# Spectral filter beside a Mish layer: eviction order and PSUM banks of the first layer

## The chip, the core and the metric

The kernel runs on one core of one Trainium2 chip. The metric is the device time of one execution in microseconds. A core has five engines, each with its own instruction queue: PE (TensorE, matmuls; PEld is its loading of weights), DVE (VectorE), ACT (ScalarE), POOL (GpSimd) and SP (SyncE, which here only issues DMAs). Matmul results land in PSUM, 128 partitions of 8 banks of 512 float32 each. ACT and DVE read them from there into SBUF.

## The reference

Two branches work on x (1 x 2048 x 512, bf16) and a gate mixes them.

```python
g = sigmoid((x * gate_w).sum(-1, keepdims=True))
X = rfft2(x.astype(float32), axes=(-2, -1)) * (w_r + 1j * w_i)      # branch A
a = irfft2(X, s=(2048, 512), axes=(-2, -1)).astype(bfloat16)
h = einsum("bsd,df->bsf", x, w1) + b1                               # branch B, F = 1792
act = h * tanh(softplus(h))                                         # mish
b = einsum("bsf,fd->bsd", act, w2)
return g * a + (1 - g) * b
```

## The kernel before

**Branch A** does the two-dimensional Fourier transform as matmuls, 2048 = 64 x 32 along the rows. The steps on PE, in the order of their dependence: transposes of x (`tr`, L507 to L528), a transform along the columns (`a1`, L588 to L591), the first half of the row transform (`s1`, L609, four of them). Its result goes out to a scratch tensor in HBM and comes back in another layout (`r1w`, `r1r`, DMAs on SP). Then four rounds n = 0 to 3 of `s2` (L727, second half of the row transform), a complex product with the filter on DVE (`wm`, L738) and a combination on POOL or DVE (`wz`, L744), and `s2i` (L780, the first half of the inverse transform). A small extra step, `s2x` (L693 to L695), handles one frequency column: DVE copies and adds (`rs`, L700; `x0`), then a row of small POOL operations ends in `z0` and the copies `wc_n` (L770), which each `s2i` needs. The results of `s2i` are evicted (`e4`, helper at L439 on DVE and L440 on ACT) and go through HBM again (`r2w`, 8 DMAs; `r2r`, 8 DMAs). For each of 16 row tiles t, then: `s1i` (L811), an eviction `e5` (L439 or L440, into `misc`), `a1i` (L823), a scaling by the gate on ACT (`geo`, L828) and two sums (`ga`, L831).

**Branch B** is a layer of F = 14 blocks of 128 over four groups c of 512 rows. `layer1(c, ft)` is one unit: four matmuls of 128x512 into one PSUM bank (L565), then a mish with bias on ACT (L575) into `act[:, c % 3, ft, :]`. There are 56 units. The second layer, `mm2` (L879; L862 for the last tile), takes 14 matmuls per row tile, in two halves of seven, into banks 4 and 5 in turn. It is evicted by ACT for the first 12 tiles (L837, with the gate as a per-partition scale), and by DVE for the others (`fin`, L889 and L869).

**PSUM banks.** Branch A uses banks 0 to 3 (and 4 and 5 in `s1`; `rcw`, L658, a small correction to the filter, uses 5). Layer 1 takes banks 6 and 7 in turn; the unit (0, 2) alone takes bank 5. A unit can start when the mish that reads its bank's former contents is done.

**Row order.** x is loaded with row 16p + t on partition p of tile t, and the transposes apply a permutation (`perm`) so that the two halves of 64 columns of a tile hold even and odd partitions. The mish restores the order: it reads the bank in order and writes its output with a step of two elements. `e5` does the same for branch A.

**Order.** No order is written out by hand. Every step is a task with an engine (or a choice of two), a planned duration, what it reads and writes, and a priority. A list scheduler (`_Graph.schedule`) plays them through at build time: of the tasks that could start within 0.1 us of the earliest, it takes the one with the highest priority, then the longest remaining path. The order on each engine's queue comes from that, and so do the waits (semaphores). For a DMA, the planned transfer time is bytes over the argument `bw`; this changes the plan alone, not the transfer. Each engine's queue is then strictly in order on the chip.

Of the kernel before, what the change touches and what calls it, by code (L numbers as in the profile page):

```python
# [14 lines left out]
NFT = 14  # L15
# [288 lines left out]

NBF = 12
NWARM = 40
PR = dict(sp0=95.0, mm1c0=90.0, mm1c=88.0, mish=92.0, mm2=70.0, fin=94.0, gate=60.0, sum=60.0)


def _build(nc, A_x, A_w_r, A_w_i, B_x, B_w1, B_b1, B_w2, gate_w, out):  # L310
# [11 lines left out]
    with es:  # L322
# [7 lines left out]
        act = sb("act", [128, 3, NFT, 512], BF)  # L330
# [221 lines left out]
                tt(f"t2{t}", Tb[:, 1, t0:t0 + 2, :], yy[:, 0], yy[:, 1], ALU.subtract, 256, [("y", yi)], [("T2", t0), ("T2", t)])  # L552


        n_mm1 = [0]

        def layer1(c, ft):
            hb, prio = c % 3, PR['mm1c0'] if c == 0 else PR['mm1c'] - c
            bank = 5 if (c, ft) == (0, 2) else 6 + n_mm1[0] % 2
            n_mm1[0] += bank != 5  # L560

            def f_mm1(e, ds):
                ins = None
                for dt_ in ds:
                    ins = e.matmul(ps[:, bank, :], w1_sb[:, dt_, 128 * ft:128 * (ft + 1)], xT[:, dt_, 4 * c:4 * c + 4, :], start=(dt_ == 0), stop=(dt_ == 3))  # L565
                return ins

            for ds in (((0,), (1,), (2,), (3,)) if (c, ft) in early else ((0, 1, 2, 3),)):
                t_mm1 = pe(f"mm1_{c}_{ft}_{ds[0]}", len(ds) * mm(512), lambda e, ds=ds: f_mm1(e, ds), writes=[("bank", bank)],
                           reads=[("xT", 4 * c + i, dt_) for i in range(4) for dt_ in ds] + [("w1", ft)],  # L570
                           prio=PR['mm1c0'] + 8 - ft if (c, ft) in early else prio)
                if (c, ft, ds[0]) == (0, 0, 0):
                    G.filled = t_mm1
            G.add(f"mish_{c}_{ft}", "act", act_dur(512, True),
                  lambda e: e.activation(act[:, hb, ft, :].rearrange("p (t a b) -> p t b a", t=4, b=2), ps[:, bank, :].rearrange("p (t b a) -> p t b a", t=4, b=2),  # L575
                                         AF.Mish, bias=b1f[:, ft:ft + 1]),
                  reads=[("bank", bank), "b1f"], writes=[("act", hb, ft)], prio=PR['mish'])

# [102 lines left out]
        s2_tasks = []  # L681
# [114 lines left out]
        for tq in range(8):  # L796
            b0 = 4 * tq
            dma(f"r2r{tq}", T2r[:, b0:b0 + 4, :], scr2_r[:, b0:b0 + 4, :],
                reads=[("scr2", n, h) for n in range(4) for h in range(2)], writes=[("T2r", b0 + i) for i in range(4)],
                deps=s2_tasks[-1:], nbytes=128 * 2048)  # L800
        G.cur_prio = SP0 + 2.6
        for t in range(NT):
            bank, ts_, gb = t % 2, t % 4, t % 2

            def f_s1i(e, t=t, bank=bank):
                ptt = ps[:, bank, :].rearrange("p (bx kc n) -> p bx kc n", bx=2, kc=2)
                ins = None
                for bx in range(2):
                    b = 2 * t + bx
                    for kc in range(2):  # L810
                        ins = e.matmul(ptt[:, bx, kc, :], T2r[:, b, 128 * kc:128 * (kc + 1)], G1s[:, b, :], start=True, stop=True)  # L811
                return ins

            pe(f"s1i_{t}", 4 * mm(128), f_s1i, reads=[("T2r", 2 * t), ("T2r", 2 * t + 1), ("m1", 0), ("m1", 1)], writes=[("bank", bank)])
            evict(f"e5_{t}", 512, TT[:, ts_, :, :].rearrange("p j (a b) -> p j b a", b=2),
                  ps[:, bank, :].rearrange("p (b j a) -> p j b a", b=2, j=4), [("bank", bank)], [("TT", ts_)])

            yk = 2 + t % 2

            def f_a1i(e, ts_=ts_, yk=yk):  # L820
                ins = None
                for j in range(4):
                    ins = e.matmul(ps[:, yk, 256 * (j // 2):256 * (j // 2) + 256], TT[:, ts_, j, :], GDs[:, j, :], start=(j % 2 == 0), stop=(j % 2 == 1))  # L823
                return ins

            pe(f"a1i_{t}", 4 * mm(256), f_a1i, reads=[("TT", ts_), "GD"], writes=[("bank", yk)])
            G.add(f"geo_{t}", "act", act_dur(512, True),
                  lambda e, t=t, gb=gb, yk=yk: e.activation(gEO[:, gb, :], ps[:, yk, :], AF.Copy, scale=gcol[:, t:t + 1]),  # L828
                  reads=[("bank", yk), "gcol"], writes=[("gEO", gb)])
            for (i, op) in ((0, ALU.add), (1, ALU.subtract)):  # L830
                fg = (lambda e, i=i, op=op, t=t, gb=gb: e.tensor_tensor(out=ga[:, t, 256 * i:256 * i + 256], in0=gEO[:, gb, 0:256], in1=gEO[:, gb, 256:512], op=op))  # L831
                G.add_multi(f"ga{i}_{t}", [("dve", dve_dur(256), fg), ("pool", pool_dur(256), fg)],
                            reads=[("gEO", gb)], writes=[("ga", t, i)])
# [10 lines left out]

        for c in range(NCH):
            hb = c % 3
            for ft in range(NFT):
                if (c, ft) not in early:
                    layer1(c, ft)
            G.cur_prio = PR['mm2'] - c  # L850
            for tl in range(4):
                t = 4 * c + tl
                bank = 4 + (t % 2)
                if t == NT - 1:
                    G.cur_prio = PR['mm2'] - 10
                    for i, (c0, w_) in enumerate(((0, 384), (384, 128))):
                        cs_, bk = slice(c0, c0 + w_), 1 + i

                        def f_mm2h(e, t=t, tl=tl, bk=bk, hb=hb, cs_=cs_, w_=w_):
                            ins = None  # L860
                            for ft in range(NFT):
                                ins = e.matmul(ps[:, bk, 0:w_], act[:, hb, ft, 128 * tl:128 * (tl + 1)], w2_sb[:, ft, cs_],  # L862
                                               start=(ft == 0), stop=(ft == NFT - 1))
                            return ins

                        pe(f"mm2_{t}_{i}", 14 * mm(w_), f_mm2h, reads=[("act", hb, ft) for ft in range(NFT)] + [("w2", 0), ("w2", 1)],
                           writes=[("bank", bk)])
                        G.add(f"fin_{t}_{i}", "dve", dve_dur(w_, True),
                              lambda e, t=t, bk=bk, cs_=cs_, w_=w_: e.scalar_tensor_tensor(out=xo[:, t, cs_], in0=ps[:, bk, 0:w_], scalar=omg[:, t:t + 1],  # L869
                                                                                    in1=ga[:, t, cs_], op0=ALU.mult, op1=ALU.add),  # L870
                              reads=[("bank", bk), "omg", ("ga", t, 0), ("ga", t, 1), ("x", t)], writes=[("o", t, i)], prio=PR['fin'])
                        dma(f"out{t}_{i}", ov[:, t, cs_], xo[:, t, cs_], reads=[("o", t, i)], nbytes=128 * 2 * w_, is_out=True,
                            queue=("sp", "act")[i], prio=PR['fin'])
                    continue
                for part in range(2):
                    def f_mm2(e, t=t, tl=tl, bank=bank, part=part, hb=hb):
                        ins = None
                        for ft in range(7 * part, 7 * part + 7):
                            ins = e.matmul(ps[:, bank, :], act[:, hb, ft, 128 * tl:128 * (tl + 1)], w2_sb[:, ft, :],  # L879
                                           start=(ft == 0), stop=(ft == NFT - 1))  # L880
                        return ins

                    pe(f"mm2_{t}_{part}", 7 * mm(512), f_mm2,
                       reads=[("act", hb, ft) for ft in range(7 * part, 7 * part + 7)] + [("w2", part)], writes=[("bank", bank)])
                if t < NBF:
                    evict_b(t, bank)
                else:
                    G.add(f"fin_{t}", "dve", dve_dur(512, True),
                          lambda e, t=t, bank=bank: e.scalar_tensor_tensor(out=xo[:, t, :], in0=ps[:, bank, :], scalar=omg[:, t:t + 1],  # L889
                                                                           in1=ga[:, t, :], op0=ALU.mult, op1=ALU.add),  # L890
                          reads=[("bank", bank), "omg", ("ga", t, 0), ("ga", t, 1)], writes=[("x", t), ("o", t)], prio=PR['fin'])
                    if t == NT - 2:
                        store(t, t + 1)
                    elif t % 2 == 1:
                        store(t - 1, t + 1)
# [113 lines left out]
```

## Time and profile before

| | |
|---|---|
| runs, median (lowest to highest) | 141.21 us (140.84 to 141.6, three runs) |
| profiled execution: time | 141.44 us |
| profiled execution: span, first to last instruction | 139.7 us |
| granted TensorE clock, mean | 1.000 |
| PE busy | 132.9 us (95%) |
| PEld busy | 67.3 us (48%) |
| DVE busy | 87.6 us (63%) |
| ACT busy | 88.3 us (63%) |
| POOL busy | 36.7 us (26%) |

The page gives, for one execution, each engine's busy time, and the chain of work that ended last: followed back from the last instruction, at each step to what released it. By engine that chain is PE 78%, ACT 11%, DMA 6%, issue 2%, DVE 1%. "Issue" is time in which an engine waited for nothing that the profile shows. A group of instructions is given as its line, engine, operation, output and input tiles, shapes and count, then after the bar its busy time in us and the mean of one in ns, then the engine's idle time just before them and what ended most of it. A busy PE isn't PE at its best: matmuls are pipelined, so one of 512 columns is shown as 380 ns although they follow one another every 0.216 us.

Busy time by stretch (us from the start of the span; PE, DVE and ACT busy us):

| stretch | what runs | PE | DVE | ACT |
|---|---|---|---|---|
| 8.50 to 38.85 | tr, a1, s1; units 3 to 22 of layer 1 | 29.98 of 30.35 | 22.50 | 28.85 |
| 38.85 to 60.47 | units to 43; s2_0, s2x | 20.69 of 21.62 | 14.46 | 17.48 |
| 60.47 to 75.95 | s2i_0 to s2_2; mm2 of group 0 | 15.16 of 15.48 | 10.03 | 5.54 |
| 75.95 to 88.38 | the last 12 units; s2i_2, s2_3 | 12.13 of 12.43 | 9.62 | 10.45 |
| 93.07 to 103.88 | s2i_3, mm2, the road through HBM | 9.69 of 10.81 | 1.23 | 3.09 |
| 103.88 to 126.75 | s1i, a1i, mm2 | 22.66 of 22.87 | 20.32 | 16.90 |
| 126.75 to 139.70 | the last mm2, fins, stores | 10.56 of 12.95 | 4.60 | 0.82 |

### The profile page before, as it was taken

How to read it: one execution, taken by the hardware profiler on the slowest of the kernel's cores; microseconds unless marked ns; L12 is line 12 of the kernel's file. 1: busy time of each engine (PE TensorE's matmuls, PEld its weight loads, DVE VectorE, ACT ScalarE, POOL GpSimd, SP SyncE). 2: the span in 40 equal slices, each digit the busy share in tenths (PEclk: the TensorE clock that was granted, in tenths of full speed). 3: DMA queues.
4: the chain of work that ended last, by engine and by line, in shares of the span. 5: the costliest groups of instructions: out<-in, count | busy, mean ns of one | idle time of the engine just before them, and what ended most of it. 6: DMA issues, size and time to landing. Idle time of an engine off the chain costs nothing.

```text
span 139.7 us, 2549 instructions
## 1 busy us (share of the span) xinstructions
PE 132.9 (95%) x955; PEld 67.3 (48%) x971; DVE 87.6 (63%) x195; ACT 88.3 (63%) x124; POOL 36.7 (26%) x68
## 2 busy tenths in 40 slices
PE   6999999999999999999999999999969999999993
PEld 4646656655433333433433333434436676665452
DVE  0265777939999259436947947921005999998042
ACT  4289898989989878751066897533137679773000
POOL 2000494030000655234404404400002442673000
DMA  4999999999553956106004106003469321211021
GB/s 97 322 384 382 394 264 283 254 368 338 135 136 113 320 187 225 75 0 155 0 0 115 35 5 152 0 0 83 147 197 292 112 77 75 80 75 75 0 105 47
DMA packets 18920, 21.32 MB, mean 153 GB/s; under 512 B 1180, under 2 KB 16284, under 8 KB 18524
## 3 DMA queue, kind: packets, MB, share of 16 engines
q1 hardware_dynamic: 17872, 17.19, 39.7%
q0 software_dynamic: 864, 3.94, 9.6%
q8 instruction: 7, 0.11, 0.4%
q10 hardware_dynamic: 172, 0.04, 0.1%
q14 instruction: 5, 0.04, 0.1%
HBM read 14.87 MB, written 6.29 MB: 151 GB/s over the span
## 4 chain that ended last, share of the span: by engine, by line
PE 78%; ACT 11%; DMA 6%; issue 2%; DVE 1%; SPq 0%
PE ps L565 27%; PE ps L879 26%; ACT act L575 8%; PE ps L823 5%; DMA Abuf<-scr 3%; PE ps L497 3%; PE ps L609 3%; PE ps L811 3%; DMA scr<-Ybuf 2%; PE ps L862 2%; PE ps L591 2%; PE ps L528 2%; PE ps L727 2%; PE ps L780 1%; ACT Ybuf L440 1%
## 5 line engine op out<-in xcount | busy, mean ns | idle before, releaser
L565 PE MATMUL ps<-xT,w_sb 128*128 128x512 bf16 x215 | 53.2, 380 | 1.5 <-issue 0.3
L575 ACT ACTIVATE act<-ps,b1f 128x512 bf16<-128x512 f32 x56 | 46.3, 837 | 7.0 <-PE ps L565 5.7
L879 PE MATMUL ps<-w_sb,act 128*128 128x512 bf16 x203 | 46.8, 379 | 0.6 <-issue 0.2
L565 PEld LDWEIGHTS ps<-xT,w_sb 128*128 128x128 bf16 x224 | 19.2, 98 | 28.3 <-ACT act L575 10.7
L879 PEld LDWEIGHTS ps<-w_sb,act 128*128 128x128 bf16 x210 | 20.0, 98 | 23.4 <-issue 1.7
L738 DVE TENSOR_TENSOR misc<-ps,WT 128x512 f32<-128x512 f32 x32 | 19.8, 680 | 7.8 <-PE ps L727 7.8
L837 ACT ACTIVATE xo<-ps,omg 128x512 bf16<-128x512 f32 x12 | 8.2, 687 | 18.6 <-PE ps L879 18.6
L831 POOL TENSOR_TENSOR Tg<-misc 128x256 bf16<-128x256 f32 x12 | 10.1, 846 | 26.4 <-ACT misc L828 26.4
L744 POOL TENSOR_TENSOR misc<-misc 128x255 bf16<-128x255 f32 x16 | 11.3, 729 | 19.8 <-DVE misc L738 19.8
L439 DVE CAST Ybuf<-ps 128x512 bf16<-128x512 f32 (+1 forms) x10 | 8.8, 901 | 10.6 <-PE ps L780 9.1
L831 DVE TENSOR_TENSOR Tg<-misc 128x256 bf16<-128x256 f32 x20 | 13.4, 699 | 0.8 <-ACT misc L828 0.8
L439 DVE CAST misc<-ps 128x512 bf16<-128x512 f32 x8 | 5.8, 727 | 11.0 <-PE ps L811 11.0
L828 ACT ACTIVATE misc<-ps,gcol 128x512 f32<-128x512 f32 x16 | 10.5, 684 | 3.2 <-PE ps L823 2.5
L439 DVE COPY xT<-ps 128x512 bf16<-128x512 bf16 x14 | 5.9, 422 | 10.0 <-PE ps L528 5.1
L440 ACT ACTIVATE Ybuf<-ps 128x512 bf16<-128x512 f32 (+1 forms) x14 | 9.4, 717 | 3.4 <-PE ps L780 2.3
L631 DVE SCALAR_TENSOR_TENSOR junk<-xo,gwb 128x512 bf16<-128x512 bf16 x16 | 11.0, 690 | 0.7
L440 ACT ACTIVATE Abuf<-ps 128x512 bf16<-128x512 f32 x13 | 9.7, 743 | 0.1
L823 PE MATMUL ps<-GDs,misc 128*128 128x256 bf16 x64 | 9.4, 273 | 0.0
L440 ACT ACTIVATE misc<-ps 128x512 bf16<-128x512 f32 x8 | 6.0, 748 | 2.3 <-PE ps L811 2.3
L763 POOL TENSOR_TENSOR gexp<-gbase,gdot 128x16 f32<-128x16 f32 x1 | 2.9, 2944 | 16.4 <-DVE junk L631 16.4
L823 PEld LDWEIGHTS ps<-GDs,misc 128*128 128x128 bf16 x64 | 6.0, 98 | 2.3 <-ACT misc L440 0.2
L811 PE MATMUL ps<-m1g,Abuf 128*128 128x128 bf16 x64 | 5.7, 219 | 1.1 <-DMA Abuf<-scr 1.1
(86 smaller groups left out, 109.3 us busy)
## 6 DMA issues: line engine op xcount, KB each, us to landing
scr<-Ybuf SPq DMA_DIRECT2D x16, 256.0 KB, 3.7
Abuf<-scr SPq DMA_DIRECT2D x4, 512.0 KB, 6.3
Abuf<-scr SPq DMA_DIRECT2D x8, 256.0 KB, 4.9
w_sb<-in_B_w_dram POOLq DMA_DIRECT2D x2, 896.0 KB, 12.7
out_dram<-xo SPq DMA_DIRECT2D x7, 256.0 KB, 2.0
w_sb<-in_B_w_dram SPq DMA_DIRECT2D x3, 512.0 KB, 8.2
xo<-in_A_x_dram SPq DMA_DIRECT2D x3, 512.0 KB, 9.1
WT<-in_A_w_r_dram POOLq DMA_DIRECT2D x4, 257.0 KB, 6.4
```

The costliest lines, as they stand in the source:

```text
L439: G.add_multi(name, [("dve", dve_dur(n, rate=rate), lambda e: e.tensor_copy(out=dst, in_=src)), ("act", act_dur(n), lambda e: e.activation ...
L440: ("act", act_dur(n), lambda e: e.activation(dst, src, AF.Copy))],
L565: ins = e.matmul(ps[:, bank, :], w1_sb[:, dt_, 128 * ft:128 * (ft + 1)], xT[:, dt_, 4 * c:4 * c + 4, :], start=(dt_ == 0), stop=(dt_ == 3))
L575: lambda e: e.activation(act[:, hb, ft, :].rearrange("p (t a b) -> p t b a", t=4, b=2), ps[:, bank, :].rearrange("p (t b a) -> p t b a", t ...
L631: lambda e, t=t: e.scalar_tensor_tensor(out=junk[:, :], in0=xo[:, t, :], scalar=1.0, in1=gwb[:, :], op0=ALU.mult, op1=ALU.mult, accum_out= ...
L738: lambda e, Pb=Pb, Wu=Wu, h=h, uu=uu, pb=pb: e.tensor_tensor(out=Pb[:, pb, :].rearrange("p (c j m) -> p c j m", c=2, j=2), in0=ps[:, 2 * h ...
L744: fz = (lambda e, c=c, Pb=Pb, op=op, pb=pb, h=h, uu=uu, zb=zb: e.tensor_tensor(out=Zb[:, zb, h, c, uu, 1:256], in0=Pb[:, pb, 1:256], in1=P ...
L811: ins = e.matmul(ptt[:, bx, kc, :], T2r[:, b, 128 * kc:128 * (kc + 1)], G1s[:, b, :], start=True, stop=True)
L823: ins = e.matmul(ps[:, yk, 256 * (j // 2):256 * (j // 2) + 256], TT[:, ts_, j, :], GDs[:, j, :], start=(j % 2 == 0), stop=(j % 2 == 1))
L828: lambda e, t=t, gb=gb, yk=yk: e.activation(gEO[:, gb, :], ps[:, yk, :], AF.Copy, scale=gcol[:, t:t + 1]),
L831: fg = (lambda e, i=i, op=op, t=t, gb=gb: e.tensor_tensor(out=ga[:, t, 256 * i:256 * i + 256], in0=gEO[:, gb, 0:256], in1=gEO[:, gb, 256:5 ...
L879: ins = e.matmul(ps[:, bank, :], act[:, hb, ft, 128 * tl:128 * (tl + 1)], w2_sb[:, ft, :], start=(ft == 0), stop=(ft == NFT - 1))
```

## The change

The mish and `e5` now write their output in order and read the PSUM bank with a step of 64 floats. The units (1, 10) to (2, 13) of layer 1 take the banks 6, 7, 4, 5 in turn. So that the second layer of group 0, which also uses banks 4 and 5, comes after them, the units of groups 0, 1 and 2 are added to the graph before it (the units of group 3 before the second layer of group 1). Within a group, units have falling priority by ft. The planned rate of the first `r2r` DMA goes from 300e3 to 110e3 bytes per us.

```diff
+WIDE = ((1, 10), (2, 13))
...
-        n_mm1 = [0]
+        n_mm1, n_wide = [0], [0]
...
-            bank = 5 if (c, ft) == (0, 2) else 6 + n_mm1[0] % 2
-            n_mm1[0] += bank != 5
+            if (c, ft) == (0, 2):
+                bank = 5
+            elif WIDE[0] <= (c, ft) <= WIDE[1]:
+                bank = (6, 7, 4, 5)[n_wide[0] % 4]
+                n_wide[0] += 1
+            else:
+                bank = 6 + n_mm1[0] % 2
+                n_mm1[0] += 1
...
-                           prio=PR['mm1c0'] + 8 - ft if (c, ft) in early else prio)
+                           prio=PR['mm1c0'] + 8 - ft if (c, ft) in early else prio - 0.01 * ft)
...
-                  lambda e: e.activation(act[:, hb, ft, :].rearrange("p (t a b) -> p t b a", t=4, b=2), ps[:, bank, :].rearrange("p (t b a) -> p t b a", t=4, b=2),
+                  lambda e: e.activation(act[:, hb, ft, :].rearrange("p (t a b) -> p t a b", t=4, b=2), ps[:, bank, :].rearrange("p (t b a) -> p t a b", t=4, b=2),
                                          AF.Mish, bias=b1f[:, ft:ft + 1]),
...
-                deps=s2_tasks[-1:], nbytes=128 * 2048)
+                deps=s2_tasks[-1:], nbytes=128 * 2048, bw=110e3 if tq == 0 else 300e3)
...
-            evict(f"e5_{t}", 512, TT[:, ts_, :, :].rearrange("p j (a b) -> p j b a", b=2),
-                  ps[:, bank, :].rearrange("p (b j a) -> p j b a", b=2, j=4), [("bank", bank)], [("TT", ts_)])
+            evict(f"e5_{t}", 512, TT[:, ts_, :, :].rearrange("p j (a b) -> p j a b", b=2),
+                  ps[:, bank, :].rearrange("p (b j a) -> p j a b", b=2, j=4), [("bank", bank)], [("TT", ts_)])
...
-            for ft in range(NFT):
-                if (c, ft) not in early:
-                    layer1(c, ft)
+            for cc in {0: (0, 1, 2), 1: (3,)}.get(c, ()):
+                for ft in range(NFT):
+                    if (cc, ft) not in early:
+                        layer1(cc, ft)
```

In the instruction order that the scheduler makes of it, the matmuls of the second layer and of layer 1 keep their number. Twelve units instead of eleven stand between `rcw` and s2_0, six instead of seven between s2_0 and s2x; the unit (1, 11) stands before (1, 10), and (3, 1) before (3, 0). Between s2i_3 and the first `s1i` stand 49 second-layer matmuls instead of 42, and at the end, after the last `a1i`, 28 of 128x512 instead of 35. For n = 0, POOL does five `wz` instead of four and DVE three, and DVE's `rs` and `x0` come before its two small gate operations (`gcol`, `omg`). The added lines of the file move line numbers by seven or eight: L565 becomes L572, L575 becomes L582, L811 becomes L818, L879 becomes L887.

## The prediction

> **What bounds the kernel now.** I read the page first: PE is busy for 95% of the 139.7 us span, so what can be saved is time in which PE waits, plus whatever another engine makes it wait. The table of stretches gives a granted clock of 1.00 in each of them. Then I read the chain that ended last, in order of time (start, length, what; lines between are left out):
>
> ```profile
> 38.85 1.05 PE ps L565 x4
> 39.92 0.85 ACT act L575
> 40.77 0.05 issue
> 40.82 1.05 PE ps L565 x4
> ...
> 49.71 0.56 PE ps L727 x16
> ...
> 60.47 0.59 PE ps L780 x16
> ...
> 77.02 0.84 ACT act L575
> ...
> 88.54 4.53 PE ps L879 x21
> 93.07 0.62 PE ps L780 x16
> 93.71 1.24 DVE Ybuf L439
> 95.01 0.57 SPq L409
> 95.59 0.05 issue
> 95.64 3.37 DMA scr<-Ybuf
> ...
> 99.09 4.74 DMA Abuf<-scr
> 103.88 0.62 PE ps L811 x8
> ```
>
> There are two places. From 38.85 to 60.47, PE (one layer-1 unit, L565) and ACT (its mish, L575) alternate on the chain. A bank is written in 1.05, read in 0.85 and released in about 0.07, a cycle of 1.97 us. Two banks are in turn, so a unit leaves every 0.98 us, while its four matmuls need only 0.863 (21 matmuls in 4.53 us, 0.216 each). The second place is the road by DMA from the last s2i (93.07) to the first s1i (103.88), 10.81 us. PE's timeline shows an idle of 1.07 us at its end, released by "DMA Abuf<-scr".
>
> Next, the groups of instructions, with shapes kept apart; the second number after the bar is the mean in ns:
>
> ```profile
> L575 ACT ACTIVATE act<-ps,b1f 128x512 bf16<-128x512 f32 x56 | 46.3, 837 | 7.0 <-PE ps L565 5.7 <-PE ps L879 0.6
> L837 ACT ACTIVATE xo<-ps,omg 128x512 bf16<-128x512 f32 x12 | 8.2, 687 | 18.6 <-PE ps L879 18.6
> L440 ACT ACTIVATE Abuf<-ps 128x512 bf16<-128x512 f32 x13 | 9.7, 743 | 0.1
> L440 ACT ACTIVATE Ybuf<-ps 128x512 bf16<-128x512 f32 x10 | 5.3, 596 | 1.0 <-PE ps L609 0.9
> L440 ACT ACTIVATE Ybuf<-ps 128x1024 bf16<-128x1024 f32 x4 | 4.1, 1020 | 2.3 <-PE ps L780 2.3
> ```
>
> These four 128x512 rows make a square. Without a per-partition operand, a contiguous write takes 596 and a write to every second element 743. With such an operand, a contiguous write takes 687. Mish, strided and with the operand, takes 837. The stride costs 147 or 150, the operand 91 or 94, the function nothing.
>
> Last, the side work behind the first s2i, on DVE and POOL:
>
> ```profile
> 55.80 0.74 DVE L744 TENSOR_TENSOR misc<-misc 128x255 bf16<-128x255 f32 x2
> 57.63 0.17 DVE L700 COPY rs<-ps 128x4 f32<-128x4 f32 x1 [0.72 <-PE ps L695]
> 60.15 0.35 POOL L770 COPY misc<-z 128x8 bf16<-128x8 bf16 x2
> ```
>
> DVE waited 0.72 for s2x (L695), and POOL's copies end just before s2i_0 at 60.47. Once PE is faster, this chain is what can come late.
>
> **The change part by part.** *Mish and e5 write in order and read PSUM with a step of 64 floats.* The 56 mishes lose the 150 ns of the strided write and gain what the strided read costs. No ACT row here reads PSUM with a step. From below, 687 is the floor: the same shape, operand and output, read in order. From above, one more pass over the elements: (1020-596)/512 = 0.83 ns an element, 425 ns, so 1.11 us. The nearest row is ACT's copy of bf16 PSUM into xT: 128x512 in 594, as long as 596 for float32. ACT thus gets nothing from narrower elements lying closer in PSUM; it goes element by element. I take a free read, 0.69. e5 (16 evictions, 748 on ACT, 727 on DVE) falls to about 0.60 on ACT and 0.68 on DVE, and since PE runs from 103.88 to 126.75 with 22.66 of 22.87 busy, I cost it at nothing. Its cover is PE's own work there.
>
> A rule weighed: the Trainium skill, "Advanced Engine Details and Errata", section "PSUM Cachelines", says that lines there hold 8 bytes and that any non-contiguous pattern significantly slows matmuls. If that held for ACT's reads too, the sum would be that of the slower rival below. Its "SBUF Cachelines" asks for two hits in a 16-byte line for full speed; every second bf16 gives four, so by that rule the strided write was free and nothing is saved. The rows say 147, and the measurement decides.
>
> *The first 22 units (8.5 to 38.85).* Their order is unchanged. ACT is busy 28.85 of 30.35 us and loses 22 x 0.15 = 3.3, but only PE's waits can be won. In the chain: 0.17 at 20.49 (a 0.06 matmul took 0.23), 0.25 between 24.52 and 28.73 where the chain runs over ACT, 0.10 at 31.40, and some 0.3 in smaller ones. That makes 0.8, part of it DVE's or the loads'. I take 0.4, with ends of 0 and 0.8.
>
> *Four banks and the new order (38.85 to 60.47).* Before, banks 4 and 5 stand empty here once the small correction at 38.8 (L658) has been read; the second layer needs them only from 62. In the instruction order of the changed kernel the first four units still use banks 6 and 7, and (1,11) and (1,10) change places. Then the rotation 4, 5, 6, 7 has each unit wait for the mish four units back. ACT starts a mish every 0.68 when it isn't waiting (two in 1.35 at 26.73), below 0.863, so PE never waits. Twelve units instead of eleven stand before s2_0, and six instead of seven between it and s2x. Third unit: 38.85 + 1.05 + 0.69 + 0.07 = 40.66. Ten units of 0.863: s2_0 at 49.29 (before 49.71). Its data come from four DMAs issued from 42.70 on, the quickest landing in 4.0: not the bound. s2x: 49.29 + 0.56 + 0.16 + 6 x 0.863 = 55.19 (before 57.13). Its last DMA had landed by 52.45, when SP went on.
> The side chain: DVE follows s2_0 0.42 earlier, ends its eight products at 55.4 and, with one Z instead of two, is free at 55.8; s2x would allow 55.19 + 0.50 = 55.7. POOL's fifth Z (0.7) starts at 55.4 and is done before it is needed, at 56.6. From the first rs copy to s2i_0 went 2.84 us, on POOL's small operations, of which I keep 2.8: s2i_0 at 58.6. PE would be there at 55.19 + 0.41 + 0.16 + 2.59 = 58.35, so this chain is late next, by 0.25. Gain: 60.47 - 58.6 = 1.9. Were mish still 0.84, ACT would still keep up at two in 1.70, and the gain would be 1.7.
>
> *Last layer-1 block (76.1 to 88.54), still two banks.* Twelve units, one s2i, one s2 need 10.36 + 0.57 + 0.72 = 11.65 of 12.45: 0.8 of waits. With mish at 0.69 a pair cycles in 1.81 against 1.73 of work, instead of 1.97: two thirds go, 0.5.
>
> *r2r0's planned rate, 110e3.* It alters no transfer, only the planner's idea of when r2r0 lands. It puts seven more second-layer matmuls (7 x 0.216 = 1.51) ahead of s1i_0. PE's work in the DMA road grows from 9.74 to 11.25, more than 10.81: the 1.07 us go. The end has as many fewer (28 for 35), so nothing is added. The margin is 0.4. If the DMA road is longer than that, the rest is paid. SP's queue order is the same before and after. On DVE the first fin now stands behind two ga's of 0.7 each; PE needs its bank only after another 2.4 us, which hides them.
>
> *prio - 0.01*ft* shows only in the order already counted.
>
> Sum: 0.4 + 1.9 + 0.5 + 1.1 = 3.9 us. The profiled execution took 141.44 (span 139.7), so 137.5, with a span of 135.8. The median of the runs, 141.21, is 0.23 lower and would give 137.3. I say 137.4.
>
> **The rivals.** *The read costs what the write saved* (mish stays near 0.84). For it: two strided sides of one kind of copy. Against it: the bf16 row. Only the four banks and the longer cover pay: 1.7 + 1.0 = 2.7, so 138.6.
>
> *Side chains eat the gain*: z0 on POOL comes later than reckoned (1.0 lost), and the DMA road runs 1 us longer (0.7 lost). For it: margins of 0.25 and 0.4, the smallest in the sum. Against it: the rows of both chains, which the change doesn't touch. 3.9 - 1.7 = 2.2, so 139.1.
>
> *Slower: the strided read takes a second pass, mish 1.11.* It strikes in the first 38.85 us, where ACT is full. 22 x 0.27 = 6 us more on ACT, two thirds of it on the path, 4.0. The last block's pair cycle goes from 1.97 to 2.23, five times 0.26 = 1.3. The wide stretch becomes ACT's, at 0.96 a unit (1.11 less the 0.15 by which ACT overlaps two), and gains nothing; the DMA cover still gives 1.0. 4.0 + 1.3 - 1.0 = 4.3 slower, so 145.6. From 0.84 each 0.1 us of mish costs about 2 us, against 2.7 gained: it decides from a mish of about 0.97.
>
> *The change doesn't do what it says*: the four banks could stand in the code and the planner not use them. The built order shows that it does, so I give it nothing.
>
> **How the numbers follow.** A measurement can tell about 0.5% (0.7 us) here. Forecast 0.60, read as dear as the write 0.14, side chains 0.10: all faster, 0.84. Slower by the read 0.12. A read in between, near 0.95, ends within the bound: 0.04. Range: the low end takes every part at its best (0.8 + 2.0 + 0.8 + 1.1 = 4.7, from the median 136.5, say 136.4); the high end takes in both faster rivals, 139.4. What it leaves out is the slower case, the even one, and little else.
>
> **What would show it.** Right: L575 near 690 ns and e5 near 600 on ACT; the chain from 40 to 58 on PE alone, s2_0 near 48.9, s2i_0 near 58.2; no idle before the first L818 (s1i); span near 135.8. Wrong: L575 at 840 (first rival) or over 970 (slower), ACT lines on the chain before 38; PE waiting on POOL's small copies before s2i_0, or on "DMA Abuf<-scr" before s1i_0.

## The result, and the profile after

| | before | after |
|---|---|---|
| four runs each, median (lowest to highest) | 141.13 us (140.84 to 141.6) | 137.53 us (137.27 to 137.64) |
| ratio, 95% interval | | 0.9739 (0.9708 to 0.9769) |
| profiled execution, span | 139.7 us | 135.7 us |

The page after first: the groups of instructions whose durations the forecast named (line, engine, operation, output and input, shapes, count, then busy us and mean ns of one; shapes kept apart).

```profile
L582 ACT ACTIVATE act<-ps,b1f 128x512 bf16<-128x512 f32 x56 | 38.2, 688 | 10.5 <-PE ps L572 9.1 <-PE ps L887 0.6 <-PE ps L666 0.2
L440 DVE CAST misc<-ps 128x512 bf16<-128x512 f32 x8 | 5.5, 683 | 11.3 <-PE ps L818 11.3
L441 ACT ACTIVATE misc<-ps 128x512 bf16<-128x512 f32 x8 | 4.7, 594 | 0.0
```

Mish fell from 837 to 688 ns, e5 on ACT from 748 to 594, on DVE from 727 to 683. These are the numbers of an ordered read with an ordered write (687 and 596 on ACT in the rows of the prediction, 684 for DVE's ordered copies in the profile before): this stepped read costs nothing measurable. Of ACT's idle time before the mishes, 9.1 of 10.5 us now end with PE; before it was 5.7 of 7.0. ACT has more time to spare.

The chain that ended last, in order of time:

```profile
39.41 9.53 PE ps L572 x43
48.95 0.60 PE ps L734 x16
49.58 2.48 DVE misc L745 x4
...
55.45 0.08 DVE rs L707
...
57.64 0.19 POOL z L767
...
57.88 0.23 POOL misc L777
...
58.16 0.64 PE ps L787 x16
...
90.35 0.57 PE ps L787 x16
...
91.72 9.88 PE ps L887 x45
101.60 0.45 PE ps L818 x8
```

ACT has left the chain between 39.4 and s2_0 (L734): PE alone, 9.53 us for eleven units. What took its place stands right below: DVE's products, rs and the small operations on POOL, up to s2i_0 at 58.16. At the other end, the road through HBM is gone from the chain: second-layer matmuls run up to the first s1i (L818) at 101.60.

### The profile page after: what moved, and what is told of

Same layout as the page of the kernel before. It is cut to its first block, busy times and chain, and to the rows that moved or that the text cites. A ratio compares the mean times of both kernels' runs of the same rounds, so it can differ in the third digit from the quotient of the medians.

```text
span 135.7 us, 2549 instructions
## 1 busy us (share of the span) xinstructions
PE 130.8 (96%) x955; PEld 68.3 (50%) x971; DVE 86.9 (64%) x194; ACT 79.8 (59%) x124; POOL 37.4 (28%) x69
## 4 chain that ended last, share of the span: by engine, by line
PE 90%; DVE 5%; POOL 1%; issue 1%; ACT 1%
PE ps L887 33%; PE ps L572 30%; PE ps L830 5%; DVE misc L745 4%; PE ps L498 3%; PE ps L616 3%; PE ps L818 3%; PE ps L598 3%; PE ps L870 2%; PE ps L529 2%; PE ps L734 2%; PE ps L787 1%; PE ps L595 1%; PE ps L516 1%; DVE misc L751 1%
## 5 line engine op out<-in xcount | busy, mean ns | idle before, releaser
L572 PE MATMUL ps<-xT,w_sb 128*128 128x512 bf16 x215 | 51.4, 380 | 0.7 <-ACT act L582 0.2
L887 PE MATMUL ps<-w_sb,act 128*128 128x512 bf16 x203 | 46.8, 379 | 0.6 <-issue 0.2
L582 ACT ACTIVATE act<-ps,b1f 128x512 bf16<-128x512 f32 x56 | 38.2, 688 | 10.5 <-PE ps L572 9.1
L572 PEld LDWEIGHTS ps<-xT,w_sb 128*128 128x128 bf16 x224 | 20.3, 98 | 24.6 <-ACT act L582 3.8
L887 PEld LDWEIGHTS ps<-w_sb,act 128*128 128x128 bf16 x210 | 20.0, 98 | 23.4 <-issue 1.7
L838 POOL TENSOR_TENSOR Tg<-misc 128x256 bf16<-128x256 f32 x13 | 11.0, 853 | 27.1 <-ACT misc L835 27.1
L751 POOL TENSOR_TENSOR misc<-misc 128x255 bf16<-128x255 f32 x17 | 12.1, 731 | 19.4 <-DVE misc L745 19.4
L838 DVE TENSOR_TENSOR Tg<-misc 128x256 bf16<-128x256 f32 x19 | 12.7, 699 | 0.5 <-ACT misc L835 0.4
L410 POOL DMA_DIRECT2D WT<-in_A_w_r_dram x4 | 2.2, 570 | 14.0 <-DMA w_sb<-in_B_w_dram 14.0
L598 PE MATMUL ps<-FDs,Tg 128*128 128x256 bf16 x32 | 6.0, 273 | 0.0
```

What stands on the lines that cost most here:

```text
L598: ins = e.matmul(pr[:, 1], Tb[:, 2 + i, t, :], FDs[:, 256 + 256 * i:512 + 256 * i].rearrange("p (r c q) -> p r c q", r=2, c=2), start=(i = ...
L751: fz = (lambda e, c=c, Pb=Pb, op=op, pb=pb, h=h, uu=uu, zb=zb: e.tensor_tensor(out=Zb[:, zb, h, c, uu, 1:256], in0=Pb[:, pb, 1:256], in1=P ...
```

## The experiments

The theory (A) is the sum of the prediction: four separate waits of PE, each ended by one part of the change. The rivals give the whole to one part, or put the saved work somewhere it doesn't count. Times stand beside the kernel before on the same chip (141.3 to 141.4 us).

**The read order alone.** The kernel before, with

```diff
-  act[...].rearrange("p (t a b) -> p t b a", ...), ps[...].rearrange("p (t b a) -> p t b a", ...)
+  act[...].rearrange("p (t a b) -> p t a b", ...), ps[...].rearrange("p (t b a) -> p t a b", ...)
```

and the same for e5.

> The kernel before, with only the mish and e5 changed to write in order and read PSUM with a step of 64; two banks, the order of before. Theory A (the sum of the prediction): mish at 0.69 shortens the two-bank cycle from 1.97 to 1.81, so the stretch from unit 23 to s2i_0 wins about 1.4, the first units 0.4, the last layer-1 block 0.4; the 1.07 us of idle before the first s1i stay. Together 2.2 us: about 139.0 against 141.2 for the kernel before. Theory B (the banks alone carry the middle stretch, the read order only the rest): 0.8 us, 140.4. Theory C (the read order carries nearly everything, the banks are ornament): 3 us or more, 138.2 or less.

Measured: 138.79, ratio 0.9831 (0.9803 to 0.9859), 2.5 us less. The chain of this run, around the first s2i, and at the end of the DMA road:

```profile
39.45 9.04 PE ps L565 x39
...
58.74 0.64 PE ps L780 x16
...
90.94 0.62 PE ps L780 x16
...
96.97 4.22 DMA Abuf<-scr
101.19 0.05 issue
101.23 0.62 PE ps L811 x8
```

With two banks, 10 units take 9.04 us or 0.90 each (the reckoning had 1.81 / 2), and s2i_0 comes 1.73 earlier than before: 0.34 of it before unit 23, 1.39 after. The last block gives 0.40. The idle before s1i stays, at 0.56 instead of 1.07, as r2r0 landed in 4.22 us rather than 4.74; in this profile that makes the gain larger than the 2.2 reckoned. A fits, B and C don't.

**Banks, order and planned rate alone.** The changed kernel, with the two edits above taken back.

> The changed kernel with the mish and e5 of the kernel before (written with a step, read in order); four banks, new order and r2r0's planned rate kept. Theory A: mish stays at 0.84, ACT still starts one every 0.85 or less, so PE runs from unit 26 to s2x without waiting: 1.7 us there, 1.1 at the first s1i, nothing in the first units nor in the last block. Together 2.8: about 138.4. Theory B: about 137.9 (all of the middle stretch). Theory C: only the 1.1 of the cover, 140.1. If A holds, the two parts alone sum to 5.0 against 3.7 for both together, since both take away the same waits.

Measured: 138.80, ratio 0.9825 (0.9802 to 0.9848), 2.5 us less. The chain of this run:

```profile
40.13 0.85 ACT act L582
...
41.02 8.81 PE ps L572 x40
49.83 0.56 PE ps L734 x16
...
57.09 0.84 ACT act L582
...
59.04 0.64 PE ps L787 x16
```

Mish is at 838 ns, and still it doesn't stop PE between 41.02 and s2_0: ten units in 8.81. Behind s2x, where the rotation over four banks ends, one mish stands on the chain again (57.09) and costs about 0.2. From unit 23 to s2i_0 the run saves 1.6 us (reckoned 1.7), and another 1.1 to 1.2 at the first s1i; 0.2 of that isn't seen in the span, because this execution began later (first `a1` at 8.70 us instead of 8.50). The two parts give 2.5 + 2.5 alone and 3.6 to 3.9 together (the result above, and the changed kernel run again, below): they end the same waits in the middle stretch, as A had it. No run has the four banks without the new order. In both kernels 21 units stand between `rcw` and s2i_0, so the order by itself takes no work out of the stretch.

**The cover of the DMA road,** added alone to the kernel before, and taken alone from the changed one:

```diff
-                deps=s2_tasks[-1:], nbytes=128 * 2048)
+                deps=s2_tasks[-1:], nbytes=128 * 2048, bw=110e3 if tq == 0 else 300e3)
```

> The kernel before with only r2r0's planned rate changed to 110e3: 49 instead of 42 second-layer matmuls between the last s2i and the first s1i. Theory A: the 1.07 us of idle before the first s1i go and nothing comes back: 1.0 us less than the kernel before, about 140.2. Rival (the seven matmuls are missed at the end, where ga and fin then wait): no difference.

> The changed kernel with r2r0 planned at 300e3 as before: 42 second-layer matmuls instead of 49 stand between the last s2i and the first s1i. Theory A: PE comes to s1i about 1.1 us before r2r0 has landed and waits; the time is 1.1 us over the changed kernel's, about 138.6. Rival (the DMA road shortened by itself, or the seven matmuls only change places with a wait at the end): no difference from the changed kernel, 137.5.

Measured: alone 140.17, ratio 0.9914 (0.9885 to 0.9944), 1.2 less. Taken away 138.24, ratio 0.9786 (0.9759 to 0.9812), 0.7 more than the changed kernel: its six runs lie from 137.70 to 138.53, the ten of the changed kernel from 137.17 to 137.71. PE's timeline at the first s1i in three profiles without the cover (the kernel before, the read order alone, the changed kernel without it), and the chain with it, in the kernel before:

```profile
103.88 0.62 PE L811 MATMUL ps<-m1g,Abuf 128*128 128x128 bf16 x8 [1.07 <-DMA Abuf<-scr]
101.23 0.62 PE L811 MATMUL ps<-m1g,Abuf 128*128 128x128 bf16 x8 [0.56 <-DMA Abuf<-scr]
100.97 0.62 PE L818 MATMUL ps<-m1g,Abuf 128*128 128x128 bf16 x8 [1.16 <-DMA Abuf<-scr]
```

```profile
92.83 0.57 PE ps L780 x16
93.40 10.68 PE ps L879 x49
104.08 0.45 PE ps L811 x8
```

49 matmuls run without a gap where 42 ended in a wait. The wait's size varies from one execution to the next: 1.07, 0.56 and 1.16 in the three profiles. The 0.7 of the timed runs lies in that spread; A's 1.1 was the size in one profile. After a wait, the first s1i also takes 0.62 on the chain, and 0.45 where it follows other matmuls, so the cover is worth the wait and 0.17 more.

**Evictions that PE's work hides.** e5 put back to its stepped write in the changed kernel, and e1 (16 evictions into Abuf) changed to an ordered write as well:

> The changed kernel with only e5 as in the kernel before (written with a step). Theory A: e5 costs 748 on ACT instead of 594 and 727 on DVE instead of 683, and PE's own work hides it: within 0.1 us of the changed kernel, 137.5. Rival (e5 is on PE's road, since a1i waits for it): 16 evictions of 0.04 to 0.15 us, half of them exposed: 0.5 to 1 us slower, 138.0 to 138.5.

```diff
-  In1[:, t, :].rearrange("p (x q i) -> p x i q", ...), ps[...].rearrange("p (i x q) -> p x i q", ...)
+  In1[:, t, :].rearrange("p (x q i) -> p x q i", ...), ps[...].rearrange("p (i x q) -> p x q i", ...)
```

> The changed kernel, with e1 too (the 16 evictions of the column transform into Abuf) writing in order and reading PSUM with a step of 256 between pairs. Theory A: on ACT 747 becomes 0.60, on DVE 726 becomes 0.68, 2 us less work on ACT, but PE has at most some 0.4 us of waits left in the first 38.4: 137.2 to 137.5. Rival (ACT bounds the first stretch, so its work comes off the time): 1 us or more, 136.5.

Measured: e5 old 137.52, ratio 0.9739 (0.9716 to 0.9762); the changed kernel itself, run again beside another set, gave 137.47:

> The changed kernel itself, beside the others on the same chip: 137.5, all theories.

Its ratio was 0.9723 (0.9695 to 0.9750). So e5 at 745 on ACT instead of 594 costs nothing measurable. With e1 in order: 137.16, ratio 0.9704 (0.9680 to 0.9728), the lowest median of all runs, 0.3 under the changed kernel, but the intervals overlap. In its profile the e1 evictions fell from 747 to 595 ns on ACT, and from the first `a1` to `rcw` it takes 29.58 us where the changed kernel takes 29.68: 0.1 is what the profiles show of some 2 us less work on ACT.

**More banks in the last block.**

```diff
+            elif (c, ft) >= (3, 2):
+                bank = (7, 6, 4, 7, 6, 4, 7, 6, 4, 7, 6, 7)[ft - 2]
```

> The changed kernel, with the units (3, 2) to (3, 13) on three banks (7, 6 and 4 in turn) instead of two. The planner also moves some second-layer halves between the last units. Theory A (in the last block of layer 1 PE still waits 0.4 us for the two-bank cycle of 1.81): 0.4 us less than the changed kernel, about 137.1. Rival (the road over s2_3, DVE's products and s2i_3 has become the bound there): no gain, and PE waits at s2i_3.

Measured: 137.63, ratio 0.9740 (0.9710 to 0.9770): nothing won. The chain shows neither theory's picture:

```profile
71.97 7.10 PE ps L574 x32
79.08 0.57 PE ps L789 x16
79.64 1.63 PE ps L889 x7
...
81.30 0.70 ACT xo L846
82.00 0.05 issue
82.04 1.69 PE ps L889 x7
```

With the bank free, the planner sets second-layer halves between the units, and after the half that ends at 81.27 PE waits for an eviction (L846) of their bank. The rival had its wait at s2i_3 instead. From s2_2 to the last s2i this run takes 17.36 with seven second-layer matmuls fewer in it (1.51), so 18.87 with them, where the changed kernel takes 18.68: 0.2 longer, not 0.4 shorter.

The starts of the single matmuls in the two traces say why. Inside this block they follow one another every 0.216 us. In the changed kernel three steps from one unit to the next are 0.30 instead (at 75.19, 77.01 and 83.62), so the two-bank cycle still costs at most 3 x 0.08 = 0.24, not 0.4. With three banks two such steps remain (74.29 and 85.94), which wins 0.08. The step to the half that waits for L846 (from 81.44 to 82.04) is 0.60, where 0.31 is usual behind an s2: 0.29 lost. An order with the halves kept behind the units wasn't tried.

**What a step costs on either side.** The 14 mishes of group 2 with seven pairs of patterns, two each. It was run once, for its rows alone; its time isn't compared.

> The changed kernel, where the 14 mishes of group 2 read and write with seven pairs of patterns, two of each, on lines of their own, to price a step on either side by itself (the rows of group 2 therefore leave in another order than the reference's). Line 585: read step 64, write step 64. 587: read step 2, write in order. 589: read step 2, write step 2. 591: read in order (as step 1 pairs are not formed: both index orders swapped on the write alone), see below. 593: read in order, write step 4. 595: read in order, write step 8. 597: read step 8, write in order. In 585 the read is in the order of memory and only the write steps by 64; in 591 both sides step by 64. Theory A (an element of PSUM costs ACT the same wherever it lies; only the write pays): every row with an ordered write is 0.69, whatever the read; every row with a stepped write 0.84. Rival (the step of 64 is free by luck of the addresses, other steps are not): 587 or 597 above 0.75. For the write, if what counts is that neighbours don't share a word, all steps cost 0.84; if what counts is the number of hits in a 16-byte line, step 2 (four hits) and 4 (two hits) are cheaper than 8 and 64 (one).

That text names two patterns wrongly. By the code, line 585 reads and writes in order, and 591 reads in order and writes with a step of 64 (0, 64, 1, 65 and so on). The groups of this run, shapes kept apart; 598 is the mish of the changed kernel:

```profile
L598 ACT ACTIVATE act<-ps,b1f 128x512 bf16<-128x512 f32 x42 | 28.6, 689 | 6.9 <-PE ps L572 5.5 <-PE ps L904 0.6 <-PE ps L683 0.2
L591 ACT ACTIVATE act<-ps,b1f 128x512 bf16<-128x512 f32 x2 | 4.9, 2697 | 0.7 <-PE ps L572 0.7
L595 ACT ACTIVATE act<-ps,b1f 128x512 bf16<-128x512 f32 x2 | 4.8, 2654 | 0.0
L593 ACT ACTIVATE act<-ps,b1f 128x512 bf16<-128x512 f32 x2 | 2.8, 1526 | 0.0
L589 ACT ACTIVATE act<-ps,b1f 128x512 bf16<-128x512 f32 x2 | 1.7, 834 | 0.2 <-PE ps L572 0.2
L597 ACT ACTIVATE act<-ps,b1f 128x512 bf16<-128x512 f32 x2 | 1.5, 802 | 0.0
L585 ACT ACTIVATE act<-ps,b1f 128x512 bf16<-128x512 f32 x2 | 1.4, 687 | 0.4 <-PE ps L572 0.4
L587 ACT ACTIVATE act<-ps,b1f 128x512 bf16<-128x512 f32 x2 | 1.4, 687 | 0.4 <-PE ps L572 0.4
```

| pattern | read from PSUM | write to SBUF |
|---|---|---|
| in order | 687 | 687 |
| step 2 | 687 | 837 (kernel before) |
| step 4 | not run | 1526 |
| step 8 | 802 | 2654 |
| step 64, in pairs | 689 | 2697 |

The same pattern that is free to read, 0, 64, 1, 65, costs four times the time to write. And reading isn't free everywhere: a step of 8 costs 115 ns. So the rival of that text holds in part: which steps are free depends on the step.

**Where a slower mish would have turned the change over.** First with patterns, then with a bank held longer:

```diff
-  act[...].rearrange("p (t a b) -> p t a b", t=4, b=2), ps[...].rearrange("p (t b a) -> p t a b", t=4, b=2)
+  act[...].rearrange("p (t m j h) -> p t h m j", t=4, m=4, h=2), ps[...].rearrange("p (t j h m) -> p t h m j", t=4, m=4, h=2)
```

> The changed kernel, with every mish reading PSUM with a step of 8 and writing with a step of 2 (it computes all, but the rows of branch B leave in another order than the reference's). It tests the price line of the slower rival. Theory A: the two sides add, 0.69 + 0.15 + 0.12 = 0.95 us; the wide stretch is still PE's (0.95 less an overlap of 0.15 is 0.80, under 0.863), the first 22 units cost two thirds of 22 x 0.11 = 1.6 over the run with mish at 0.84 and the last block 5 x 0.11 = 0.6, so 138.8 + 2.2 = 141.0, even with the kernel before. Rival (every mish is paid in full, in the wide stretch too): 56 x 0.11 = 6 us over that run, 145. Rival (the two sides don't add, the slower hides the other): mish at 0.84 and 138.8.

Measured: 138.55, ratio 0.9793 (0.9766 to 0.9821), with the mish at 838: the slower side hides the other, so A's 0.95 never came about. The longer hold therefore came from a second instruction:

```diff
+                e.activation(pad[:, (c * NFT + ft) % 4, 0:264], ps[:, bank, 0:264], AF.Copy)
                 return e.activation(act[...], ps[...], AF.Mish, bias=b1f[:, ft:ft + 1])
```

> The changed kernel, with a copy of 264 elements of the same bank on ACT ahead of each mish (into a buffer nobody reads), so that the bank is held about 0.97 us and ACT is as busy as by a mish of 0.97. It tests the point from which the slower rival of the prediction was to decide. Theory A (the price line of the prediction: 2 us for each 0.1 above 0.84): 138.7 + 2.6 = 141.3, even with the kernel before. Rival (only the first stretch and the last block pay, and less): 139.5 to 140.5.

> The same with a copy of 432 elements: the bank is held about 1.11 us, the mish of the slower rival. Theory A: 145.6 as reckoned there, 4.3 over the kernel before. Rival (less is exposed, since the four banks also hide a held bank): 142 to 144. Rival (the wide stretch turns to ACT and stalls PE for longer than reckoned): 147 or more.

Measured: 140.60, ratio 0.9950 (0.9928 to 0.9972) at 0.97, and 144.97, ratio 1.0263 (1.0228 to 1.0298) at 1.11. On the chains the copy and the mish behind it take 0.39 + 0.58 and 0.53 + 0.58 us, so the banks were held as long as intended. At 0.97 A's 141.3 is missed by 0.7 and the rival's 139.5 to 140.5 by 0.1: from `rcw` to s2i_0 that run is still 1.2 us quicker than the kernel before. At 1.11 it lies between A's 145.6 and the rival's 144. The chain of the latter run shows the turn:

```profile
46.52 0.42 ACT pad L583
46.94 0.58 ACT act L584
47.52 0.42 ACT pad L583
```

From 46 to 61 it is ACT's alone, 1.00 us a unit (the prediction had 0.96), over PE's 0.863. A straight line between the two holds meets the kernel before (141.3) at 0.99; the prediction had 0.97. By stretches the held bank at 1.11 costs 2.6 in the first (the small correction rcw starts at 41.22 instead of 38.60; 2.9 counted from the first `a1`, as this execution began 0.26 earlier), 0.5 in the middle, 1.3 in the last block, and gets 1.2 back at the end: 3.2 of span, and 3.7 by the medians, against the 4.3 reckoned. With a bank held that long the rival's mechanism is real; its first term, 4.0, was too dear, and the middle stretch, put at nothing, cost 0.5. A single mish of 1.11 us wasn't run.

## Why the prediction was right

| step | reckoned | profile after |
|---|---|---|
| mish | 0.69 us | 0.688 |
| first 22 units | 0.4 | 0.37 (38.77 to 38.40) |
| to s2i_0 | 1.9 | 1.94 (60.47 to 58.16, less 0.37) |
| last block, to the last s2i | 0.5 | 0.41 (93.07 to 90.35, less 2.31) |
| DMA road and end | 1.1 | 1.28 (the span's 4.0 less 2.72) |
| sum | 3.9 | 4.0 |

The spans give 4.0 and the medians 3.6 (141.13 to 137.53), because the profiled execution of the kernel before was 0.3 above its median. The first row is firmer than one pair of profiles: from the first `a1` to `rcw` the four profiles with a mish of 0.84 take 30.10 to 30.11 us, the six with a mish of 0.69 and e1 as before 29.67 to 29.68, so 0.43. What differs among them is when the first `a1` starts, from 8.26 to 8.75.

*Each wait was reckoned from the stretch in which it stood.* PE is busy for 95% in the page, so its share could promise little; the chain gave what each wait was worth, and the two one-part kernels confirm that the parts overlap in the middle stretch alone.

*What comes late next was named in advance.* s2i_0 was put at 58.6 less 0.4 for the first stretch, held by POOL's small operations; in the profile it is 58.16, and the chain runs over them. PE waits 0.16 there.

*One reading was off, without consequence.* "ACT starts a mish every 0.68" was read from two mishes in 1.35 us in the kernel before, and those are the mishes of 0.84: two that follow one another overlap by 0.16. Two of 0.69 start 0.57 apart in the profile after (26.38 and 26.96). Both are under 0.863, which is why the four banks hid either.

*The reason for the free read was too wide.* The step said that ACT goes element by element and gets nothing from how elements lie in PSUM, since bf16 and float32 copies take the same time. For steps of 2 and of 64 in pairs that came true; at a step of 8 the read took 802. That the number was right is luck in part: this pattern is among the cheap ones. Of the two rules weighed, the one on PSUM lines wasn't visible in the mish, at 688 against 687 in order; whether it holds for matmuls no run here shows.

*On the write side* the rule of the Trainium skill ("Advanced Engine Details and Errata", section "SBUF Cachelines") has full speed from two hits in a 16-byte line. The order of the costs fits it: four hits (step 2) 837, two (step 4) 1526, one (step 8) 2654. The full speed doesn't: two hits already cost more than double the ordered 687.

*The rivals.* The read as dear as the write is out by the 688. The side chains took nothing beyond the 0.16. The slower rival would have needed a bank held for 0.99, by the straight line above. The last block was off by 0.1 of 0.5: at most 0.24 of its waits stayed. The last row took 0.2 more than the idle of 1.07: 0.17 of it is the first s1i, 0.62 on the chain behind a wait and 0.45 without one, a cost of the wait that the sum had left out.

## What to carry to other kernels

When an order has to be undone between PSUM and SBUF, put the step on the PSUM read and write in order, but measure that step: 64 in pairs was free here, 8 was not. Ahead of a bank count, work out the cycle of one bank (write, read, release) against the work of a unit: two banks with a cycle of 1.97 us let a unit go every 0.98 us where its work is 0.863, four banks hid a mish of either length, and the two remedies don't add where they end the same wait. And a planner's wrong idea of a transfer is worth correcting: for r2r0 the plan had 2.9 us from issue to landing (a fixed 2.0 and the bytes over the rate), the traces show 4.2 to 4.8, and the new rate makes 4.4 of it. That one number moved seven matmuls in front of a 1.07 us wait, for no work at all.

## What the runs showed of the hardware that was not expected

An ACT instruction didn't pay for both sides here: with a read step of 8 and a write step of 2 the mish took 838, as long as by the write alone.

In the run with the seven patterns, PE stood idle long enough to lose its clock. PE's timeline, and then the busy time by stretch (the columns after the window are its length, busy us and count of PE, PEld, DVE, ACT and POOL, then the granted clock, DMA share and GB/s):

```profile
55.55 1.04 PE L572 MATMUL ps<-xT,w_sb 128*128 128x512 bf16 x4 [1.27 <-ACT act L591]
...
62.81 1.89 PE L572 MATMUL ps<-xT,w_sb 128*128 128x512 bf16 x4 [3.93 <-ACT act L597]
```

```profile
56.00:58.00 2.00, 2.00 (x48) 0.91 (x47) 0.87 (x8) 2.00 (x3) 0.19 (x2) 1.00 0.15 61
...
60.00:62.00 2.00, 0.00 (x0) 0.00 (x0) 0.00 (x0) 2.00 (x3) 0.00 (x0) 0.76 0.00 0
62.00:64.00 2.00, 1.19 (x3) 0.43 (x4) 0.00 (x0) 1.32 (x3) 0.00 (x0) 0.50 0.00 0
64.00:66.00 2.00, 2.00 (x19) 0.33 (x18) 0.22 (x1) 0.22 (x1) 0.13 (x1) 0.50 0.00 0
66.00:68.00 2.00, 2.00 (x6) 0.76 (x5) 1.00 (x1) 0.80 (x1) 0.09 (x1) 0.54 0.00 0
68.00:70.00 2.00, 2.00 (x24) 0.67 (x23) 0.12 (x1) 0.00 (x0) 0.00 (x0) 1.00 0.73 159
```

An idle of 1.27 us left the clock at 1.00. In the one of 3.93 us, from 58.88 to 62.81, the clock fell before PE had work again. The same view in steps of 0.25 us has 1.00 up to 61.00 and 0.50 from 61.25 on, so it fell some 2.1 us into the idle. It stayed at 0.50 for more than four microseconds after PE had work again, and a unit's four matmuls took 1.89 us from the first start to the last end, where 1.04 is usual. The Trainium skill, "TensorE: Matmul & The Clock Gate", section "Part 1: The HAM clock gate", has the clock fall after at least one idle window of about 3.4 us. In this execution it fell after about 2.1, and the measurement decides; what sets the moment of the fall no run here shows. A wait in which the clock falls costs more than its own length.
